# First unit's inverse from blocks of 16 instead of a 32-step substitution, with its V and R turned before its E, and raw W's loads issued first

## The chip, the cores and the metric

The kernel runs on one core of a Trainium2 chip. The metric is device time in microseconds of one execution; several executions are timed and the median is given. The engines are TensorE (PE in the profile, its weight loads PEld), VectorE (DVE), ScalarE (ACT), GpSimd (POOL) and SyncE (SP), which issues most DMAs. Each engine works through its own queue in order, and engines wait for each other through semaphores.

## The reference, cut to what matters

A recurrent attention block (batch 4, 8 heads, 768 tokens, head width 40) is followed by a mixture of four experts over its output, reshaped to 3072 rows of 320.

```python
for t in range(S):
    y[:, :, t] = np.einsum('bhd,bhde->bhe', rt, state)
    Sa = np.einsum('bhde,bhe->bhd', state, at)
    state_decay = state * wt[:, :, None, :] - np.einsum('bhd,bhe->bhde', Sa, bt)
    state = state_decay + np.einsum('bhd,bhe->bhde', vt, kt)
...
x = y.transpose(0, 2, 1, 3).reshape(B * S, H * D)
p = domain_probs / (domain_probs.sum(-1, keepdims=True) + 1e-09)
for e in range(E):
    h = np.maximum(x @ w1[e], 0.0)
    out += p[:, e:e + 1] * (h @ w2[e])
```

All data are float32.

## The kernel before

The sequence is cut into 12 chunks of 64 tokens. A *unit* is one chunk of two of the four batches (partitions 0 to 63 are the tokens of one, 64 to 127 of the other), so there are 24 units; units 0 and 1 are the first chunk. Within a chunk the recurrence is written with matrices: a unit needs the inverse of a unit triangular matrix of 64x64 for each head and batch.

For one unit the work goes in three generators and one function.

`within(q)` (L501) does what needs no state. In order: turn raw W into G, cumulated decays by a scan (L566), pg by TensorE and the reciprocal 1/gp, N and K scaled by it, NT and KT, the products pfe (F, the matrix to be inverted, L664 and L670) and pe (E), then E masked into ET (L686 to L697), then pev and its copies EV (L702 to L708), and for unit 0 last the turned V and R (pVT, pRT, copied by ACT to VT and RT) with the product pc, masked into VC. It yields between these, so that the main program can set other work between two pieces. For units 0 to 3 most of DVE's operations in it are kept in program order.

`substitute(q, ...)` (L717) inverts the two diagonal 32x32 blocks of F for all 8 heads. The blocks are copied side by side, turned into M so that a partition holds one matrix, and 32 columns are eliminated two at a time: sixteen pairs, each a multiplication (L760) and, on DVE, a reduction over three terms (L771), into the tile Z. Units 0 and 1 do it on DVE, later units on POOL. ACT sets the two copies of the unit matrix in Z.

`merge(q)` (L788) turns Z back into Qc and QTc (two transposes on DVE), POOL copies QTc to QT's diagonal, and two products, pY and pQ, with four small ACT copies after each, give the block below the diagonal: the level from 32 to 64.

`step(q, xT)` (L826) has the products with state: psat, pst, pxr, pdy, the result Y and the new state, and pxT, which puts Y into the layout of the mixture. After it the mixture's products follow (ph, po), which read the pieces of w1 (`load_piece`) and w2 (`load_w2`).

The order of PE's instructions is the program's order in the whole first part, as each matmul is kept in program order. `keep_warm(n)` puts n products of the identity with itself into that queue; nothing reads them. On DVE, POOL and SP only what passes through `keep`, `pin`, `keep_in_program_order` or a stated dependence is ordered; the rest is placed by the framework's scheduler. The third weight piece has a stated dependence on unit 0's Y.

The main program (L1217 on) for unit 0: sixteen fillers, W turned, scan, ten fillers, reciprocal, unit 1's G, loads of units 1 and 2 and of weights, N, K, NT, KT, pfe, pe, twenty fillers, the substitution (with the masked E inside), pev, transposes of Z, pVT, pRT, pc, eight fillers, the gate's transposes pp (`normalize`), unit 1's pVT, fifteen fillers, pY, unit 1's pRT, scan and pg, pQ, then `step`.

Raw W is loaded in four DMAs, two issued by SP and two by ACT. Its columns from 48 to 79 are first set to 1.0 in all partitions by a memset (L197, L218); two of the four DMAs write into those columns. PSUM has eight banks: five slots "big" and three "mm".

Of the kernel before, what the change touches and what calls it, by code (L numbers as in the profile page):

```python
# [8 lines left out]
I32 = mybir.dt.int32  # L9
# [24 lines left out]
def kernel(  # L34
# [55 lines left out]
    def noted(ins, name, n=None, i=None):  # L90
        if n is None:
            n = sum(k.startswith(name) for k in made)
        key = f"{name}{n}" if i is None else f"{name}{n}.{i}"
        made[key] = ins
        if key in names:
            stated_order.append(ins)
        return ins

    def keep(ins):

        if not any(ins is x for x in stated_order):
            tc.keep_in_program_order(ins)
# [38 lines left out]
            )  # L141
    mask_up = const.tile([P, L], I32, name="mask_up")

    def dealt(x):

        return x.rearrange("p h (k g) -> p k g h", g=4)
# [46 lines left out]
    def kept(name, shape, n, value=0.0, eng=nc.gpsimd, lo=0):  # L193
        tiles = []
        for i in range(n):
            t = const.tile(shape, FP32, name=f"{name}{i}")
            eng.memset(t[:, :, lo:shape[2]], value)  # L197
            tiles.append(t)
        turn = [0]

        def take():
            turn[0] += 1
            return tiles[(turn[0] - 1) % n]

        return take
# [9 lines left out]
        t = padded["RV"[n % 2], n // 2] = sb.tile([P, H, 64], FP32, name="padded", tag=a_sum)  # L215
        nc.gpsimd.memset(t[:, :, D:64], 0.0)
    PAD = D + D - Q
    raw = {x: kept(f"raw{x}", [P, 2 * NJ, 2 * D], 1, float(x == "W"), nc.vector, PAD) for x in "WARV"}  # L218
    room = {x: const.tile([P, 2 * NJ, 2 * D], FP32, name=f"raw{x}") for x in "BK"}
    raw.update((x, lambda t=t: t) for x, t in room.items())  # L220

# [63 lines left out]
    def load_raw(q, names):  # L285


        moves = []
        for x in names:
            q.n["raw" + x] = t = raw[x]()  # L290
            heads = srcs[x].rearrange("b h t e -> (b h) t e")[q.b[0] * H:(q.b[1] + 1) * H, q.c * L:(q.c + 1) * L, :]
            heads = heads.rearrange("n (x two) e -> x n (two e)", two=2)
            for r in range(2):
                if x in "RV":

                    sets = ((slice(0, 8, 2), slice(r, 16, 4)), (slice(1, 8, 2), slice(3 - r, 16, 4)))
# [136 lines left out]
    def half(s):  # L433
        return slice(64 * s, 64 * s + 64)
# [4 lines left out]
    def of_slot(x, s):  # L439

        return x.rearrange("p (j s) e -> p j s e", s=2)[:, :, s, :]
# [59 lines left out]
    def within(q):  # L501
# [178 lines left out]
        if not q.apart:  # L680
# [24 lines left out]
        ))  # L705
        for i in range(2):
            for p in range(2):
                nc.scalar.copy(out=of_slot(q.EV[half(p)], i ^ p)[:, :, 0:D], in_=pev[i][half(p)])  # L708
        yield

        if q.u == 0:
            pc = causal_scores(turn_rv())
            yield
            masks(pc)
        yield

    def substitute(q, eng, between=None, during=None, first=None):  # L717

# [69 lines left out]
    def merge(q):  # L788


        Qc = sb.tile([P, H, Q], FP32, name="Qc", tag="q", bufs=2)
        QTc = sb.tile([P, H, Q], FP32, name="QTc", tag="q", bufs=2)
        keep(noted(nc.vector.transpose(out=dealt(Qc[:]), in_=q.Z), "Qc", q.u))
        ins = nc.vector.transpose(  # L794
            out=QTc[:].rearrange("p h r -> p (h r)"), in_=Qc[:].rearrange("p h c -> p (h c)"),
        )
        keep(noted(ins, "QTc", q.u))
        q.QT = QTs()
        for i in range(P // Q):
            ins = nc.gpsimd.tensor_copy(out=q.QT[quarter(i), :, quarter(i % 2)], in_=QTc[quarter(i)])  # L800
            tc.keep_in_program_order(ins)
        yield

        def two_heads(name, lhsT, rhs, to):
            p = (of_mixture if q.u == 0 and name == "pY" else big)(name)
            for n in range(NJ):
                for r in range(2):
                    matmul(
                        out=p[half(r), n * 2 * Q:(n + 1) * 2 * Q], lhsT=lhsT[half(r), 2 * n:2 * n + 2, :],
                        rhs=rhs[half(r), 2 * n:2 * n + 2, :], start=True, stop=True,  # L810
                    )
            for r in range(2):
                for y in range(2):
                    src = p[quarter(2 * r + y), 0:H * Q].rearrange("p (n two t) -> p n two t", two=2, t=Q)[:, :, y, :]
                    with sooner(name == "pY"):
                        ins = nc.scalar.copy(out=of_slot(to[quarter(2 * r)], y), in_=src)
# [428 lines left out]
    substitute(units[0], nc.vector, scores_of(0))  # L1245
    run(ws[0], 1)
    set_pick()
    m, s = merge(units[0]), begin_step(0)
    run(m, 1)
    run(ws[0], 1)  # L1250
    keep_warm(8)
    run(norm, 1)
    run(ws[1], 1)
    keep_warm(15)
    load(units[2], "W")
    for x in "VR":
        load_padded(units[2], x)
# [194 lines left out]
    for one, then in [*zip(names, names[1:]), *((f"out{n}", x) for n, x in moved), ("blocks0.3", "VCv1"), ("blocks0.3", "ETc0.0"), ("blocks1.3", "Zu1.0"), ("blocks1.3", "Zu1.3"), *turned_ahead, *in_second, *waits_of_scalar, *ahead_of_merge]:  # L1452
# [31 lines left out]
```

## Time and profile before

| what | value |
|---|---|
| median of 3 runs | 1066.47 us (1066.34 to 1067.45) |
| profiled execution, its own time | 1067.89 us |
| profiled execution, span | 1066.1 us |
| unit 0: last matmuls of pfe and pe start before | 14.8 us |
| unit 0: M transposed | 15.94 to 17.95 us |
| unit 0: first pair of substitution | 20.10 us |
| unit 0: last reduction ends | 30.77 us |
| unit 0: Y on DVE | 41.72 us |
| unit 0: xT copy on ACT | 44.34 us |
| first products ph of the mixture | 45.68 us |

The table's times are from the start of the span, read from the timeline. A time in the span can be compared with another in the span; the time that is measured is the one of the runs, some 1 to 2 us longer than a span.

### The profile page before, as it was taken

The numbers are of one execution on the slowest core, as the hardware profiler recorded it, in microseconds if no ns is written. First come the engines' busy times: TensorE is split into PE (matmuls) and PEld (weight loads), VectorE is DVE, ScalarE is ACT, GpSimd is POOL, SyncE is SP. The second block draws the span as 40 slices with busy tenths as digits, with TensorE's granted clock in tenths as the row PEclk, the third lists the DMA queues.
The fourth block names the chain that finished last, engine by engine and source line by source line (L and its number), as shares of the span: only waits on it lengthen the run. The fifth ranks groups of instructions, "written<-read, shape, count | busy, mean of one in ns | idle before, by whom it ended". The sixth has DMA issues, their size and how long they took to land.

```text
span 1066.1 us, 38525 instructions
## 1 busy us (share of the span) xinstructions
PE 1049.8 (98%) x16022; PEld 942.5 (88%) x16022; DVE 802.2 (75%) x1565; ACT 344.2 (32%) x942; POOL 538.8 (51%) x1322
## 2 busy tenths in 40 slices
PE   7999999999999999999999999999999999999998
PEld 7888888888899999999999999999989998998887
DVE  7787679898778887888788788779788876634343
ACT  3432434333323324233333333232233333221110
POOL 6216777765474574563654744745745646520000
PEclk9999999999999999999999999999999999999999
DMA  6776645344443543453353453454444453121220
GB/s 114 186 211 143 147 95 121 83 98 101 107 103 83 135 109 83 113 131 81 101 135 68 104 147 73 101 115 104 108 114 100 106 109 84 60 83 37 84 78 13
DMA packets 275351, 111.05 MB, mean 104 GB/s; under 512 B 229817, under 2 KB 254953, under 8 KB 275177
## 3 DMA queue, kind: packets, MB, share of 16 engines
q1 hardware_dynamic: 271192, 107.75, 43.3%
q8 instruction: 126, 2.06, 0.8%
q10 hardware_dynamic: 3984, 0.84, 0.4%
q14 instruction: 49, 0.39, 0.1%
HBM read 100.65 MB, written 3.93 MB: 98 GB/s over the span
## 4 chain that ended last, share of the span: by engine, by line
PE 81%; POOL 8%; DVE 5%; issue 2%; DMA 2%; SPq 1%; ACT 1%; DVEq 0%; POOLq 0%; ACTq 0%
PE ph L110 36%; PE p L110 29%; POOL Z L777 5%; POOL Z L760 3%; PE pdy L110 3%; PE prn L110 2%; PE po L110 2%; PE pxr L110 2%; PE psat L110 2%; PE pfe L110 1%; PE pc L110 1%; DVE M L730 1%; PE pev L110 1%; PE pe L110 1%; PE pQ L110 1%
## 5 line engine op out<-in xcount | busy, mean ns | idle before, releaser
L777 POOL TENSOR_TENSOR Z<-Z 128x31 f32<-128x31 f32 (+7 forms) x704 | 265.6, 377 | 55.1
L110 PE MATMUL ph<-xT,w1b 128*128 128x256 f32 (+3 forms) x1536 | 222.3, 374 | 0.5 <-issue 0.5
L110 PE MATMUL ph<-xT,w1a 128*128 128x256 f32 (+3 forms) x1536 | 220.8, 373 | 0.0
L978 ACT ACTIVATE hs<-ph 128x512 f32<-128x512 f32 (+1 forms) x208 | 117.0, 564 | 319.6 <-PE ph L110 317.9
L1104 DVE TENSOR_TENSOR a<-hs 128x512 f32<-128x512 f32 x220 | 155.3, 724 | 81.8 <-ACT hs L978 81.8
L760 POOL TENSOR_TENSOR Z<-M,Z 128x62 f32<-128x62 f32 (+7 forms) x352 | 155.9, 443 | 94.9 <-DVE M L746 69.1
L110 PEld LDWEIGHTS ph<-xT,w1b 128*128 128x128 f32 (+1 forms) x1536 | 168.7, 161 | 27.8 <-issue 7.0
L110 PEld LDWEIGHTS ph<-xT,w1a 128*128 128x128 f32 (+1 forms) x1536 | 167.9, 161 | 28.3 <-issue 7.7
L110 PE MATMUL p<-sums,a 128*128 128x160 f32 x1056 | 164.9, 299 | 0.0
L993 DVE SCALAR_TENSOR_TENSOR osb<-p,gate,osb 128x320 f32<-128x320 f32 (+1 forms) x243 | 107.6, 480 | 69.4 <-PE p L110 66.2
L110 PEld LDWEIGHTS p<-sums,a 128*128 128x128 f32 x1056 | 152.8, 190 | 2.2
L727 POOL COPY below<-F 32x256 f32<-32x256 f32 x48 | 20.7, 432 | 184.0 <-ACT F L670 182.4
L110 PEld LDWEIGHTS p<-w,hs 128*128 128x128 f32 x704 | 98.6, 190 | 8.7 <-issue 7.5
L110 PE MATMUL p<-w,hs 128*128 128x160 f32 x704 | 104.9, 302 | 0.1
L110 PE MATMUL p<-w,a 128*128 128x160 f32 x704 | 102.8, 299 | 0.0
L110 PEld LDWEIGHTS p<-w,a 128*128 128x128 f32 x704 | 98.0, 190 | 0.0
L800 POOL COPY QT<-QTc 32x256 f32<-32x256 f32 x96 | 40.5, 422 | 61.1 <-DVE QTc L794 50.7
L898 ACT COPY RS<-pxr 64x256 f32<-64x256 f32 x88 | 32.3, 367 | 104.6 <-DVE SX L499 76.0
L582 DVE RECIPROCAL gp<-G 128x512 f32<-128x512 f32 x16 | 53.6, 3352 | 0.5
L708 ACT COPY EV<-pev 64x160 f32<-64x160 f32 x96 | 23.1, 286 | 83.6 <-PE pev L110 83.2
L730 DVE STREAM_TRANSPOSE M<-blocks 128x1024 f32<-128x1024 f32 x24 | 47.4, 1974 | 3.4 <-ACT blocks L722 3.3
L670 ACT COPY F<-pfe 128x256 f32<-128x256 f32 x48 | 15.5, 376 | 80.1 <-PE pfe L110 77.9
(167 smaller groups left out, 1419.3 us busy)
## 6 DMA issues: line engine op xcount, KB each, us to landing
w1a<-in_moe_w_dram SPq DMA_DIRECT2D x37, 512.0 KB
w1b<-in_moe_w_dram SPq DMA_DIRECT2D x37, 512.0 KB
w<-in_moe_w_dram SPq DMA_DIRECT2D x4, 1280.0 KB
w1a<-in_moe_w_dram SPq DMA_DIRECT2D x74, 64.0 KB
w1b<-in_moe_w_dram SPq DMA_DIRECT2D x74, 64.0 KB
out_dram<-osb SPq DMA_DIRECT2D x45, 80.0 KB
rawW<-in_w_dram SPq DMA_DIRECT2D x48, 72.0 KB
natV<-in_v_dram SPq DMA_DIRECT2D x42, 80.0 KB
```

What stands on the lines that cost most here:

```text
L110: return stated(nc.tensor.matmul(**k))
L582: pin(noted(nc.vector.reciprocal(out=gp[:], in_=G[:, :, 1:L + 1]), "1/gp", q.u))
L708: nc.scalar.copy(out=of_slot(q.EV[half(p)], i ^ p)[:, :, 0:D], in_=pev[i][half(p)])
L727: tc.keep_in_program_order(nc.gpsimd.tensor_copy(out=q.below[quarter(i)], in_=q.F[quarter(i), :, 0:Q]))
L730: ins = nc.vector.transpose(out=M[:], in_=cols)
L760: ins = eng.tensor_tensor(out=Z[:, 1:3, 0:n, j + 1:Q], in0=M[:, j:j + 2, None, j + 1:Q].to_broadcast([P, 2, n, m]), in1=Z[:, here, 0:n, j: ...
L777: eng.tensor_tensor(out=z[:, 0], in0=z[:, 0], in1=z[:, x], op=ALU.add)
L800: ins = nc.gpsimd.tensor_copy(out=q.QT[quarter(i), :, quarter(i % 2)], in_=QTc[quarter(i)])
L898: nc.scalar.copy(out=RS[half(s), x ^ s::2], in_=prs[x][half(s)].rearrange("p (j i) t -> p j i t", i=2),)
L978: ins = nc.scalar.activation(out=h[:, i * HF // 2:(i + 1) * HF // 2, 0:n], in_=ph[i][:], func=ACTF.Relu,)
L993: ins = nc.vector.scalar_tensor_tensor(out=to, in0=p, scalar=sc, in1=to, op0=ALU.mult, op1=ALU.add)
L1104: ins = nc.vector.tensor_tensor(out=t[:], in0=x, in1=y, op=op)
```

## The change

Only unit 0 is treated differently: `substitute_small` takes the place of `substitute`. It inverts the four 16x16 diagonal blocks (eight column pairs in eight steps of multiplication and reduction on tiles half as long), and `merge` puts a level before the one it has: W = inner * QTc, then QTc and Qc get a product added (32x32 products, one for each head and quarter of the partitions). `set_bands` makes the masks and scales that this needs, and half of the unit matrix; they lie in a tile `small`. V and R of unit 0 are turned, and pc computed, before E is masked; the fillers are dealt out anew (4, 16, 12, 18 in place of 20, 8, 15). Raw W gets a tile whose ones are set only in the partitions where no DMA writes those columns. The gate's normalization and two weight pieces stand later in the program.

```diff
+    T = Q // 2
+    small = sb.tile([P, 512], FP32, name="small", tag="step", bufs=3)
...
+    def set_bands():
+        nc.vector.reduce_sum(out=of_rows, in_=ident[:].rearrange("p (i b r) -> p b i r", i=2, r=T), axis=AX.XY)
+        nc.vector.tensor_copy(out=band, in_=of_rows[:, :, None].to_broadcast([P, 4, T]))
+        nc.vector.reduce_sum(out=lane_x, in_=ident[:].rearrange("p (a x h) -> p x a h", x=2, h=H), axis=AX.XY)
+        nc.vector.tensor_copy(out=lanes_of_second, in_=lane_x[:, 1:2, None].to_broadcast([P, 1, T]))
+        diag = diagf[:, 0:T].rearrange("p (k g) -> p k g", g=2)[:, :, :, None]
+        nc.vector.transpose(out=unit_small, in_=diag.to_broadcast([P, T // 2, 2, 2 * H]))
...
-    raw = {x: kept(f"raw{x}", [P, 2 * NJ, 2 * D], 1, float(x == "W"), nc.vector, PAD) for x in "WARV"}
+    raw = {x: kept(f"raw{x}", [P, 2 * NJ, 2 * D], 1, 0.0, nc.vector, PAD) for x in "ARV"}
+    raw_w = const.tile([P, 2 * NJ, 2 * D], FP32, name="rawW")
+    for i in (1, 3):
+        nc.vector.memset(raw_w[Q * i:Q * i + Q, :, PAD:D + Q], 1.0)
...
     tc.keep_in_program_order(ins)
+    set_bands()
     for n, move in enumerate(load_raw(units[0], "W")):
...
+        if q.u == 0:
+            VT = turn_rv()
+            yield
+            pc = causal_scores(VT)
+            yield
+
         ET = ETs()
...
         if q.u == 0:
-            pc = causal_scores(turn_rv())
-            yield
             masks(pc)
...
+    def substitute_small(q, first, second):
+        K = T // 2
+        blocks = sb.tile([P, H, Q], FP32, name="blocks")[:, :, 0:T]
+        keep(nc.vector.tensor_copy(out=blocks, in_=q.F[:, :, 0:T]))
+        for n in range(1, 4):
+            keep(nc.vector.copy_predicated(
+                out=blocks, mask=band[:, n:n + 1, :].to_broadcast([P, H, T]), data=q.F[:, :, n * T:n * T + T],
+            ))
+        run(first)
+        q.below = belows()
...
+        q.inner = sb.tile([P, H, Q], FP32, name="inner", tag="step", bufs=3)
+        nc.gpsimd.memset(q.inner[:, :, T:Q], 0.0)
+        for i in range(P // Q):
+            ins = nc.gpsimd.affine_select(
...
+        for x in (0, 3):
+            nc.scalar.copy(out=z[:, x], in_=unit_small[:, :, 0:T])
+        M = sb.tile([P, Q, Q], FP32, name="M")
+        cols = blocks.rearrange("p h c -> p c h")[:, :, None, :].to_broadcast([P, T, 4, H])
+        keep(nc.vector.transpose(out=M[:, 0:T], in_=cols))
+        m = M[:, 0:T, 0:T]
+        keep(nc.vector.copy_predicated(
+            out=m, mask=lanes_of_second.to_broadcast([P, T, T]), data=M[:, 0:T, T:Q],
+        ))
...
+        for j in range(0, T, 2):
+            n, w_ = j // 2 + 1, T - 1 - j
...
+        run(second)
+        ins = nc.scalar.activation(out=q.Z[:, :, T:Q], in_=z[:, 0], func=ACTF.Copy, scale=lane_x[:, 1:2])
+        tc.add_manual_dep(ins.ins, made["EVc0.3"].ins.name, BEHIND, reason="stated order of ScalarE")
+        keep(nc.vector.tensor_scalar(out=q.Z[:, :, 0:T], in0=z[:, 0], scalar1=lane_x[:, 0:1], scalar2=None, op0=ALU.mult))
...
     def merge(q):
...
+        def of_blocks(name, lhsT, rhs):
+            p = of_mixture(name)[:, 0:H * Q].rearrange("p (h c) -> p h c", c=Q)
+            for h in range(H):
+                for i in range(P // Q):
+                    o = quarter(i)
+                    matmul(out=p[o, h, :], lhsT=lhsT[o, h, :], rhs=rhs[o, h, :], start=True, stop=True)
+            return p
+
+        if q.u == 0:
+            W = sb.tile([P, H, Q], FP32, name="inner_Q", tag="step", bufs=3)
+            tc.keep_in_program_order(nc.scalar.copy(out=W[:], in_=of_blocks("pW", q.inner, QTc)))
+            yield
+            for name, to, lhsT, rhs in (("pQTc", QTc, Qc, W), ("pQc", Qc, W, Qc)):
+                p = of_blocks(name, lhsT, rhs)
+                keep(nc.vector.tensor_tensor(out=to[:], in0=p, in1=to[:], op=ALU.add))
         q.QT = QTs()
...
     load_w2(order_of(-1)[0])
-    load_piece()
-    load_piece()
     run(ws[0], 2)
-    keep_warm(20)
+    keep_warm(4)
+    run(ws[0], 1)
+    keep_warm(16)
+    run(ws[0], 1)
+    keep_warm(12)
...
-    substitute(units[0], nc.vector, scores_of(0))
-    run(ws[0], 1)
+    substitute_small(units[0], scores_of(0), scores_of(0))
     set_pick()
+    keep_warm(18)
     m, s = merge(units[0]), begin_step(0)
     run(m, 1)
+    run(ws[1], 1)
     run(ws[0], 1)
-    keep_warm(8)
-    run(norm, 1)
-    run(ws[1], 1)
-    keep_warm(15)
+    run(m, 1)
     load(units[2], "W")
...
     run(m)
     go(load_raw(units[2], "A"))
+    load_piece()
+    load_piece()
     run(s, 3)
+    run(norm, 1)
     run(ws[1], 1)
```

The two stated orders of DVE that named unit 0's blocks go as well (ahead of unit 1's V copy and of the copy of E).

More of the change, by code (lines that the diff above doesn't have):

```diff
@@ L142 @@
     mask_up = const.tile([P, L], I32, name="mask_up")
+    T = Q // 2
+    small = sb.tile([P, 512], FP32, name="small", tag="step", bufs=3)
+    unit_small = small[:, 0:T // 2 * Q].rearrange("p (k r) -> p k r", r=Q)
+    band = small[:, 256:320].bitcast(I32).rearrange("p (b r) -> p b r", r=T)
+    lanes_of_second = small[:, 320:336].bitcast(I32)[:, None, :]
+    lane_x, of_rows = small[:, 336:338], small[:, 340:344]
+    def set_bands():
[5 more added lines that the diff above has]
+        nc.vector.transpose(out=unit_small, in_=diag.to_broadcast([P, T // 2, 2, 2 * H]))
     def dealt(x):
@@ L217 @@
     PAD = D + D - Q
-    raw = {x: kept(f"raw{x}", [P, 2 * NJ, 2 * D], 1, float(x == "W"), nc.vector, PAD) for x in "WARV"}
+    raw = {x: kept(f"raw{x}", [P, 2 * NJ, 2 * D], 1, 0.0, nc.vector, PAD) for x in "ARV"}
+    raw_w = const.tile([P, 2 * NJ, 2 * D], FP32, name="rawW")
+    for i in (1, 3):
+        nc.vector.memset(raw_w[Q * i:Q * i + Q, :, PAD:D + Q], 1.0)
+    raw["W"] = lambda: raw_w
     room = {x: const.tile([P, 2 * NJ, 2 * D], FP32, name=f"raw{x}") for x in "BK"}
@@ L707, in within @@
             for p in range(2):
-                nc.scalar.copy(out=of_slot(q.EV[half(p)], i ^ p)[:, :, 0:D], in_=pev[i][half(p)])
+                ins = nc.scalar.copy(out=of_slot(q.EV[half(p)], i ^ p)[:, :, 0:D], in_=pev[i][half(p)])
+                noted(ins, "EVc", q.u, 2 * i + p)
         yield
         if q.u == 0:
-            pc = causal_scores(turn_rv())
-            yield
             masks(pc)
         yield
+    def substitute_small(q, first, second):
[8 more added lines that the diff above has]
+        q.below = belows()
+        for i in (1, 3):
+            tc.keep_in_program_order(nc.gpsimd.tensor_copy(out=q.below[quarter(i)], in_=q.F[quarter(i), :, 0:Q]))
+        q.inner = sb.tile([P, H, Q], FP32, name="inner", tag="step", bufs=3)
+        nc.gpsimd.memset(q.inner[:, :, T:Q], 0.0)
+        for i in range(P // Q):
+            ins = nc.gpsimd.affine_select(
+                out=q.inner[quarter(i), :, 0:T], in_=q.F[quarter(i), :, quarter(i % 2)][:, :, 0:T],
+                pattern=[[0, H], [0, T]], compare_op=ALU.is_ge, fill=0.0, base=-T, channel_multiplier=1,
+            )
+            tc.keep_in_program_order(ins)
+        Z = sb.tile([P, 4, Q // 4, Q], FP32, name="Z")
+        flat = Z[:].rearrange("p x k r -> p (x k r)")
+        z = flat[:, 0:4 * K * T].rearrange("p (x k r) -> p x k r", k=K, r=T)
+        for x in (0, 3):
[7 more added lines that the diff above has]
+        ))
+        pairs = M[:, 0:T].rearrange("p (c two) r -> p c two r", two=2)[:, :, :, 0:T]
+        cells = M[:, 0:T].rearrange("p c r -> p (c r)")
+        keep(nc.vector.memset(cells[:, Q + 1::2 * (Q + 1)], 0.0))
+        by_second = z[:, 1:3].rearrange("p x k r -> p (x k r)")[:, 0:K * T].rearrange("p (k r) -> p k r", r=T)
+        keep(nc.vector.tensor_tensor(
+            out=by_second, in0=pairs[:, :, 1, :],
+            in1=cells[:, 1::2 * (Q + 1)][:, :, None].to_broadcast([P, K, T]), op=ALU.mult,
+        ))
+        keep(nc.vector.tensor_tensor(out=pairs[:, :, 0, :], in0=pairs[:, :, 0, :], in1=by_second, op=ALU.add))
+        for j in range(0, T, 2):
+            n, w_ = j // 2 + 1, T - 1 - j
+            here = 3 * (j // 2 % 2)
+            nc.vector.tensor_tensor(
+                out=z[:, 1:3, 0:n, j + 1:T], in0=M[:, j:j + 2, None, j + 1:T].to_broadcast([P, 2, n, w_]),
+                in1=z[:, here, 0:n, j:j + 2].rearrange("p k x -> p x k")[:, :, :, None].to_broadcast([P, 2, n, w_]),
+                op=ALU.mult,
+            )
+            now = z[:, :, 0:n, j + 1:T]
+            terms = now[:, 0:3] if here == 0 else now[:, 1:4]
+            nc.vector.tensor_reduce(
+                out=now[:, 3 - here], in_=terms.rearrange("p x k r -> p k r x"), op=ALU.add, axis=AX.X,
+            )
+        odd, even = (z[:, x].rearrange("p k (r four) -> p k r four", four=4)[:, :, :, 1:3] for x in (3, 0))
+        nc.vector.tensor_copy(out=even, in_=odd)
+        q.Z = flat[:, 4 * K * T:4 * K * T + K * Q].rearrange("p (k r) -> p k r", r=Q)
+        run(second)
+        ins = nc.scalar.activation(out=q.Z[:, :, T:Q], in_=z[:, 0], func=ACTF.Copy, scale=lane_x[:, 1:2])
+        tc.add_manual_dep(ins.ins, made["EVc0.3"].ins.name, BEHIND, reason="stated order of ScalarE")
+        keep(nc.vector.tensor_scalar(out=q.Z[:, :, 0:T], in0=z[:, 0], scalar1=lane_x[:, 0:1], scalar2=None, op0=ALU.mult))
@@ L792, in merge @@
         QTc = sb.tile([P, H, Q], FP32, name="QTc", tag="q", bufs=2)
-        keep(noted(nc.vector.transpose(out=dealt(Qc[:]), in_=q.Z), "Qc", q.u))
+        place = Qc[:].rearrange("p h (x c) -> p c x h", x=2) if q.u == 0 else dealt(Qc[:])
+        keep(noted(nc.vector.transpose(out=place, in_=q.Z), "Qc", q.u))
         ins = nc.vector.transpose(
@@ L1451 @@
     in_second = [("Zr1.14", "out0"), ("out0", "Zm1.16")]
-    for one, then in [*zip(names, names[1:]), *((f"out{n}", x) for n, x in moved), ("blocks0.3", "VCv1"), ("blocks0.3", "ETc0.0"), ("blocks1.3", "Zu1.0"), ("blocks1.3", "Zu1.3"), *turned_ahead, *in_second, *waits_of_scalar, *ahead_of_merge]:
+    for one, then in [*zip(names, names[1:]), *((f"out{n}", x) for n, x in moved), ("blocks1.3", "Zu1.0"), ("blocks1.3", "Zu1.3"), *turned_ahead, *in_second, *waits_of_scalar, *ahead_of_merge]:
         tc.add_manual_dep(made[then].ins, made[one].ins.name, BEHIND, reason="stated order of VectorE")
```

## The prediction

> **What bounds it now.** First I read the busy shares on the page, then the waits of the PE queue, then the timeline of the first 46 us. Columns in the timeline are start, duration, engine, line, operation, out<-in, count, and in brackets the idle time before it with what ended it.
>
> ```profile
> PE 1049.8 (98%) x16022; PEld 942.5 (88%) x16022; DVE 802.2 (75%) x1565; ACT 344.2 (32%) x942; POOL 538.8 (51%) x1322
> q8 instruction: 126, 2.06, 0.8%
> ```
>
> PE is idle for 1066.1 - 1049.8 = 16.3 us, and the waits listed up to 46 us add up to 7.8 of them. From 41 us on, unit 0's results and the experts' weights keep PE full, so what the change gains or loses until unit 0's pxT is passed on to the end. The path to be watched is therefore PE's own queue, fillers ("warm") included, since its order is written out.
>
> ```profile
> 1.76 6.11 PE L110 MATMUL warm<-ident 128*128 128x128 f32 x32 [1.76 <-POOL ident L128]
> 8.14 0.66 PE L113 MATMUL pg<-ident,G 128*128 128x128 f32 x4 [0.27 <-DVE G L566]
> ...
> 14.41 0.65 ACT L670 COPY F<-pfe 128x256 f32<-128x256 f32 x2 [0.31 <-PE pfe L110]
> ...
> 14.78 4.73 PE L110 MATMUL warm<-ident 128*128 128x128 f32 x40
> ...
> 19.44 0.81 PE L110 MATMUL pev<-VC,ET 64*64 64x40 f32 x32
> ...
> 28.74 3.51 PE L110 MATMUL warm<-ident 128*128 128x128 f32 x30
> ...
> 31.48 0.45 DVE L794 STREAM_TRANSPOSE QTc<-Qc 128x256 f32<-128x256 f32 x1
> 31.84 1.18 DVE L566 TENSOR_TENSOR_SCAN G<-G,first 128x512 f32<-128x512 f32 x1
> ...
> 32.18 0.68 PE L110 MATMUL pY<-QTc,below 64*64 64x64 f32 x16
> ...
> 32.96 1.07 ACT L816 COPY Yq<-pY 32x128 f32<-32x128 f32 x4 [2.90 <-PE pY L110]
> ...
> 33.28 0.60 PE L113 MATMUL pg<-ident,G 128*128 128x128 f32 x4
> ...
> 33.81 0.95 PE L110 MATMUL pQ<-Yq,Qc 64*64 64x64 f32 x16
> ```
>
> To be seen: twenty fillers fill 14.78 to 19.44, 0.233 us each. The last fifteen end at 32.2, just as QTc comes (31.93): fillers and substitution are level at pY. Unit 1's pg stands in PE's queue between pY and pQ and needs unit 1's scan.
>
> **Raw W first, bands.** The second rawW issue on SP moves from 2.27 to about 1.4, so G's transposes (5.64, released by a DMA) could start near 4.8. set_bands adds two sums, two copies and a transpose on DVE: about 2x0.25 + 0.17 + 0.1 + 0.45 = 1.2 us (rows of total, mask_up, gl, unit_cols), hidden in DVE's 1.88 idle us before G; without that cover the same 1.2 is on the path. But pg cannot start before the sixteen fillers end at 7.87: gain 0.27, and pe starts at 13.91, F is ready at 14.8.
>
> **Shorter substitution.** On DVE: copy 0.22, three predicated copies 128x128 at about 0.25 (0.38 for 128x256), M transpose half of 2.01, predicated copy 0.38, memset 0.07, two operations at 0.24: 2.9 with gaps. A pair of steps now costs 0.47 (16 elements) to 0.67 (108); eight pairs of 16 to 72 elements give 0.49+0.53+0.57+0.59+0.59+0.55+0.51+0.47 = 4.3, against 10.7 for the sixteen (20.10 to 30.77). Z is done at 22.4. Its scaling on ACT is put behind EV's copies, which follow pev; the W and Yq copies queue behind it on ACT.
>
> **PE's queue.** From pe's end at 14.51: fifty fillers at 0.233 = 11.65; pVT and pRT 0.95; pc 0.6; pev 0.74 (19.44 to pVT at 20.18): pW starts at 28.45. pev comes at 23.5, EV's copies end at 25.3 (1.8 after pev, as before), the scaling at 25.6, Qc and QTc (0.63+0.04+0.45) at 26.8. So the fillers, not the substitution, release pW; 1.4 us of the saving stand unused, and nothing of DVE's 6.4 reaches the path but the start of this queue. Fillers at 0.229 to 0.240 (the rows of 30 and 20) move it by 0.3. POOL's below, inner (four selects at 0.28, 6.61/24, and a memset) and ET selects end about 21, covered by pev's place; VT's and RT's copies (2.27) by the sixteen fillers.
>
> **The new level.** Products of 32x32 are not in the trace. pfe's sixteen 64-wide calls show as 32 matmuls in four-tile batches, 0.51 us for eight batches; pst, 40 wide, has the same pace. Between half that pace (width counts) and double, I take the same: 32 calls are sixteen batches, 0.93 us, and 0.36 more until a reader starts (pY: 0.78 to the Yq copy, of which 0.46 to its last matmul). pW 28.45, W copy 29.74 to 30.1 (0.38), pQTc 30.15, add 31.44 to 31.84, pQc to 32.05, its add 32.37 to 32.75, pY 32.2: level with before. But unit 1's scan, kept in order, now stands behind both adds: 32.75 to 33.95, so pg 34.0 and pQ 34.55 instead of 33.81: **+0.74**. Half pace makes this -0.8, double pace +3.6.
>
> A rule speaks against this level: the Trainium skill, "TensorEngine Tiling (Array Packing)", Restrictions and Gotchas, says that different row tiles cannot use one PSUM bank at the same time, and of_blocks writes four row tiles into one bank. The trace does not bear it out: pY's two row tiles share a bank, and its 16 matmuls start two by two.
>
> **Code for PE.** The page's 32044 PE instructions over 126 packets are 254 a packet. This stop has no releaser:
>
> ```profile
> 41.01 0.30 PE L110 MATMUL pdy<-SX,n_tok 64*64 64x104 f32 x1 [0.86 <-issue]
> ```
>
> Counting back 256 (a call shows as two loads and two matmuls): pdy 80, pxr 64, pst 64, psat 48, to about 35.9; another 256 to 23.65 in pc, another to 14.1. The DMA view has a packet of the instruction queue in 38.0 to 38.9 and none in 36.0 to 38.4; one in 24.0 to 24.6; one in 14.9 to 15.6. So a block is asked for when the one before it is entered, and came 5 us later at 35.9, where DMA was busiest; from the packet to the resumption 2.5, hence 3 at 23.65. In the new order the borders lie in the twelve fillers (22.2), in pW's last quarter (29.2), and 256 later in pQc: pW 30, pVT 8, pQTc 128, pQc 90, at 31.7. That is 2.5 us for a block that takes 3 to 5: a wait of 0.5 to 2.5. DMA share there is 0.79 to 0.88, nearer to 1.05 at 35.9 than to 0.19 after 23.65: I take 4.2, a wait of **1.7**, which holds up pQc, pY, both adds and what hangs on them. The next borders fall at pxr and pc, some 5 us apart, so pdy's stop goes: **-0.86**.
>
> **Moved work.** pp (0.65) goes into PE's 0.61 wait for SX; its gate copy is 0.24 on ACT; without that cover 0.65. The weight pieces already waited on SP for Y (42.50 after 41.72), ahead of rawA, rawB, rawK; nothing is used from them before 56.2. Masks move into DVE's idle time before the adds. I put these at 0.
>
> **Sum.** +0.74 + 1.7 - 0.86 = +1.6 us, the 0.27 and the fillers already in it. The profiled execution took 1067.89 (span 1066.1 and 1.8 around it) and would take 1069.5; the median of the runs is 1066.47, which gives **1068.1**.
>
> **Rivals.**
> B, code comes in time: the block takes 3 us and waits 0.3 to 0.5, pdy's stop is gone: +0.74+0.5-0.86 = +0.4, **1066.9**. For it: most borders show no stop. Against: dense small products are where the one stop is. The Trainium skill, "Runtime: NRT & Kernel Launch", Instruction fetch mechanics, holds that crossing a 16 KiB border is mostly hidden; by that rule the time is this one, and the stop at 41.01 is a row against it.
> C, the substitution decides as it says: PE is at pW by the time Z's chain ends without EV (22.4+0.25+1.12+0.25 = 24.1), 4.3 earlier: 1068.1 - 4.3 = **1063.8**. For it: DVE's sum. Against: it needs fillers under (24.1-14.51-2.29)/50 = 0.146 us.
> D, slower, the clock. Columns: busy time of PE, PEld, DVE, ACT, POOL (and count), granted clock, DMA share, GB/s.
>
> ```profile
> 9.98:13.39 3.41, 2.08 (x18) 1.71 (x16) 3.38 (x5) 1.72 (x5) 3.00 (x9) 1.00 0.70 116
> 20.22:23.63 3.41, 1.41 (x22) 1.04 (x19) 3.03 (x12) 3.17 (x10) 0.00 (x0) 1.00 0.63 118
> 23.63:27.04 3.41, 3.41 (x36) 3.29 (x37) 3.14 (x9) 0.00 (x0) 0.00 (x0) 0.50 0.19 49
> 30.46:33.87 3.41, 3.41 (x42) 3.06 (x41) 3.31 (x10) 0.86 (x4) 1.77 (x3) 1.00 0.88 264
> ```
>
> PE busy for 1.41 of 3.41 was followed by 3.41 us at half clock, 2.08 was not. My new order leaves about 2.0 in 30.46 to 33.87; under some 1.8 half a window is lost, 1.7 us: **1069.8**.
> E: the four row tiles take turns: 64 matmuls at 0.058 are 3.7 us for each of the three products, 2.8 more than the sum has, 8.4 in all: **1076**. No row speaks for it, only the rule cited above.
>
> **Chances.** Forecast 0.46, B 0.20, C 0.17, D 0.14, E 0.03. A difference under 0.2% (2.1 us) is about what a measurement of this kernel cannot tell from none, so slower begins at 1068.6. The forecast's own range is 1066.9 to 1069.7, and nearly half of it (0.24) lies beyond. Faster: C, 0.17. Within: 0.22 + 0.20 = 0.42. Slower: 0.24+0.14+0.03 = 0.41. The range 1064.3 to 1070.5 leaves out C's fast half, E and the tails.
>
> **What would show it.** Right: pW directly behind the last filler near 28.4 with QTc a microsecond older; a PE stop without releaser in pQc or pY; scan behind two adds and pg waiting for it; no stop in pdy. Wrong: PE waiting for QTc before pW, products much off 0.93 us, unit 0's xT copy earlier than 44.34.

## The result, and the profile after

The changed kernel takes 1073.41 us (median of 6 runs, 1072.16 to 1074.79), the kernel before on the same chip 1067.62 (6 runs, 1066.34 to 1068.56): ratio 1.0056, 95% interval 1.0043 to 1.0069. It is slower by 5.8 us, where 1.6 were forecast, and lies above the range. The profiled execution is the fastest of the six, 1072.16 with a span of 1070.4: 4.3 us more than the profiled one of before.

The page's busy line of the changed kernel:

```profile
PE 1053.2 (98%) x16228; PEld 945.7 (88%) x16228; DVE 797.4 (74%) x1561; ACT 343.6 (32%) x942; POOL 537.8 (50%) x1327
```

PE idles for 17.2 us (1070.4 - 1053.2), 0.9 more than before, and is busy for 3.4 more. Most of the loss is made in one place of the timeline (columns as in the prediction):

```profile
7.43 0.60 PE L113 MATMUL pg<-ident,G 128*128 128x128 f32 x4
...
13.55 0.65 ACT L691 COPY F<-pfe 128x256 f32<-128x256 f32 x2 [0.31 <-PE pfe L110]
...
22.95 0.68 PE L110 MATMUL pev<-VC,ET 64*64 64x40 f32 x32
23.56 4.29 PE L110 MATMUL warm<-ident 128*128 128x128 f32 x36
...
25.77 0.45 DVE L884 STREAM_TRANSPOSE QTc<-Qc 128x256 f32<-128x256 f32 x1
27.77 0.75 PE L110 MATMUL pW<-QTc,inner 32*32 32x32 f32 x64
29.05 0.72 PE L110 MATMUL pQTc<-inner_Q,Qc 32*32 32x32 f32 x62
...
29.62 0.68 PE L110 MATMUL pQc<-Qc,inner_Q 32*32 32x32 f32 x41
29.98 0.42 DVE L903 TENSOR_TENSOR QTc<-pQTc,QTc 128x256 f32<-128x256 f32 x1 [3.10 <-PE pQTc L110]
35.10 0.53 PE L110 MATMUL pQc<-Qc,inner_Q 32*32 32x32 f32 x21 [4.80 <-issue]
35.56 1.12 PE L110 MATMUL pY<-QTc,below 64*64 64x64 f32 x16
35.68 0.42 DVE L903 TENSOR_TENSOR Qc<-pQc,Qc 128x256 f32<-128x256 f32 x1 [5.28 <-PE pQc L110]
36.02 1.21 DVE L587 TENSOR_TENSOR_SCAN G<-G,first 128x512 f32<-128x512 f32 x1
37.52 1.06 PE L113 MATMUL pg<-ident,G 128*128 128x128 f32 x4
38.51 1.12 PE L110 MATMUL pQ<-Yq,Qc 64*64 64x64 f32 x16
...
48.07 0.48 ACT L1042 COPY xT<-pxT 128x384 f32<-128x384 f32 x1 [0.81 <-PE pxT L110]
```

Until 30.3 all goes as planned or better: Z's transposes end at 26.22, the fillers at 27.85, pW follows at once, and 64 products of 32x32 are started in some 0.56 us (0.75 with the last one's end). Then PE stands in the middle of pQc, after 43 of its 64 matmuls, for 4.80 us, waiting for nothing that the profile shows. Behind the stop the same operations take longer: pY 1.12 where it took 0.68, pg 1.06 where it took 0.60. The windows say why (columns: PE, PEld, DVE, ACT, POOL, granted clock, DMA share, GB/s):

```profile
30.46:33.87 3.41, 0.00 (x0) 0.00 (x0) 0.00 (x0) 0.00 (x0) 1.57 (x4) 0.91 1.10 338
33.87:37.28 3.41, 2.18 (x40) 1.99 (x40) 1.56 (x3) 0.48 (x2) 0.00 (x0) 0.50 0.65 116
```

In the first stretch PE did nothing and DMA was full; from 33.3 to 40.1 PE's granted clock was 0.5. The copy xT comes at 48.07 where it came at 44.34: 3.7 of the span's 4.3 us are lost by then.

### The profile page after: what moved, and what is told of

Read it like the earlier page. It is cut to its first block, busy times and chain, and to the rows that moved or that the text cites. A ratio compares the mean times of both kernels' runs of the same rounds, so it can differ in the third digit from the quotient of the medians.

```text
span 1070.4 us, 38944 instructions
## 1 busy us (share of the span) xinstructions
PE 1053.2 (98%) x16228; PEld 945.7 (88%) x16228; DVE 797.4 (74%) x1561; ACT 343.6 (32%) x942; POOL 537.8 (50%) x1327
## 4 chain that ended last, share of the span: by engine, by line
PE 83%; POOL 10%; DVE 3%; issue 2%; ACT 1%; DMA 1%; SPq 0%; POOLq 0%; DVEq 0%
PE ph L110 35%; PE p L110 29%; POOL Z L866 6%; POOL Z L849 3%; PE pdy L110 3%; PE prn L110 2%; PE po L110 2%; PE pxr L110 2%; PE psat L110 2%; PE pfe L110 1%; PE pc L110 1%; PE warm L110 1%; PE pev L110 1%; PE pe L110 1%; PE pQ L110 1%
## 5 line engine op out<-in xcount | busy, mean ns | idle before, releaser
L866 POOL TENSOR_TENSOR Z<-Z 128x31 f32<-128x31 f32 (+7 forms) x704 | 272.3, 387 | 55.1
L849 POOL TENSOR_TENSOR Z<-M,Z 128x62 f32<-128x62 f32 (+7 forms) x352 | 148.2, 421 | 94.6 <-DVE M L835 68.9
```

The source lines that it names most:

```text
L849: ins = eng.tensor_tensor(out=Z[:, 1:3, 0:n, j + 1:Q], in0=M[:, j:j + 2, None, j + 1:Q].to_broadcast([P, 2, n, m]), in1=Z[:, here, 0:n, j: ...
L866: eng.tensor_tensor(out=z[:, 0], in0=z[:, 0], in1=z[:, x], op=ALU.add)
```

## The experiments

Each ran beside the kernel before on the same chip; ratios are to its runs.

**The stop is code.** To show it without the change, the kernel before got 96 products of 32x32 that nothing reads, ahead of pY:

```diff
     keep_warm(15)
+    extra = of_mixture("extra")
+    for n in range(3 * H):
+        for i in range(P // Q):
+            o = quarter(i)
+            ins = matmul(out=extra[o, 0:Q], lhsT=ident[o, quarter(i)], rhs=ident[o, quarter(i)], start=True, stop=True)
+            tc.keep_in_program_order(ins)
```

> The kernel before, with 96 products of 32x32 that nobody reads set into PE's queue between the last filler and pY: PE's share of the new level by itself, without its adds and copies and without the new order of the scan. Theory 1: the products take 3x0.56 = 1.7 us of PE, and a border of the code lies near the start of pY, asked for about 2.5 us earlier; PE stops there without a releaser for 2.5 to 5 us, and the time rises by 3 to 6 us. Rival (it is the adds, copies and the order behind them that cost, not the code): no stop, +1.7 us at most.

It took 1076.18 (one run; before 1067.51): 8.7 us more, above the 3 to 6 expected; 10.2 us at half clock follow the stop. Its timeline has the stop inside products that depend on nothing:

```profile
38.93 0.42 PE L110 MATMUL extra<-ident 32*32 32x32 f32 x11 [5.06 <-issue]
```

If all PE records (matmuls, loads and the waits for semaphores between them) are counted from the start of the span, the first one behind this stop is number 962. It is 962 in the changed kernel too, and behind the stop of 0.86 in pdy of the kernel before. Three different products stop at one count, which speaks for a border in PE's instructions and against anything in the data. Borders 256 records apart put the one before at 706.

The DMA view of the changed kernel shows what PE waits for (columns: packets, MB, share of the 16 engines). From 28.3 to 32.5 there is data alone; from 32.5 to 33.6 one packet of the instruction queue:

```profile
q1 hardware_dynamic: 924, 1.33, 95.2%
...
q8 instruction: 1, 0.02, 6.0%
```

If the next block is asked for when PE enters a block, it had these times to come (start of the record behind each border and of the packet, from the traces; the three kernels with QTc transposed stop at 1218, the others at 962):

| kernel | border before, us | packet begins after | behind the border, us | between | stop |
|---|---|---|---|---|---|
| before | 36.06 | 2.40 | 41.01 | 4.95 | 0.86 |
| before, 96 products more | 32.60 | 3.33 | 38.93 | 6.33 | 5.06 |
| before, one cast more | 35.73 | 2.73 | 40.92 | 5.19 | 1.10 |
| before, new tile of raw W | 37.65 | 0.52 | 41.38 | 3.73 | none |
| changed | 28.19 | 4.32 | 35.10 | 6.91 | 4.80 |
| changed, no new level | 38.71 | 2.79 | 43.98 | 5.27 | 0.88 |
| changed, weights late | 34.45 | 2.11 | 39.03 | 4.58 | 2.49 |
| changed, w2 late | 28.19 | 3.01 | 33.70 | 5.51 | 3.43 |
| changed, casts on POOL | 29.05 | 5.26 | 36.90 | 7.85 | 5.78 |
| changed, casts on POOL, w2 late | 29.03 | 2.52 | 33.93 | 4.90 | 2.77 |
| changed, pieces put right | 27.40 | 1.96 | 31.60 | 4.20 | 1.81 |
| QTc transposed, weights late | 33.62 | 4.39 | 40.77 | 7.15 | 2.86 |
| the same, weights early | 33.89 | 4.29 | 40.81 | 6.92 | 2.63 |
| the same, w1 early, w2 late | 33.50 | 2.31 | 38.21 | 4.71 | 0.42 |

So where PE stopped, a block took 4.2 to 7.9 us from the border before to PE's going on. In each of the thirteen PE goes on 1.2 to 1.5 us after the end of the packet; in the one kernel without a stop the packet ended 2.0 us before PE was at the border. What differs is how long the packet takes to begin. (At record 450, under fillers, it begins up to 0.8 us before PE is there in eight of the profiles, so the asking can run somewhat ahead of PE.) The kernels in the other rows are told below.

Leaving the new level out moves the same count into pdy:

```diff
         if q.u == 0:
+            yield
+        if False:
             W = sb.tile([P, H, Q], FP32, name="inner_Q", tag="step", bufs=3)
```

> The changed kernel without the new level: pW, its copy, pQTc, pQc and both adds are left out, so the blocks of 16 are not joined to 32 for the first unit. Theory 1: 384 instructions fewer between the fillers and pY, no stop of code there; pY follows the fillers at 27.9 instead of 35.56, and the time falls by 7 to 9 us against the changed kernel. Rival (the stop comes anyway a block later): the fall is below 4 us.

There is no stop before pY, and one of 0.88 in pdy, at record 962. But the time was 1070.74 (one run), only 2.7 us less than the changed kernel's and not the 7 to 9 expected: pY starts at 34.98, not at 27.9. Another line shows the reason; see the cast below.

**What makes the stop long.** First the weights were moved out of the way, to behind pQ:

```diff
     load_probs()
-    load_piece()
-    load_piece()
-    load_w2(order_of(-1)[0])
...
     run(m)
+    load_piece()
+    load_piece()
+    load_w2(order_of(-1)[0])
     go(load_raw(units[2], "A"))
```

> The changed kernel with the loads of the first two weight pieces and the first w2 moved in the program from before the products of the new level to behind pQ. Theory 1: PE's stop of 4.8 us in pQc is a code block that comes late because it is asked for while these 2.5 MB are on the DMA queues. Then the stop shrinks to at most 1.5 us, no half clock follows, and the time falls by 4 to 6 us, to 1067 to 1069.5 where the changed kernel has 1073.4. Rival: the stop belongs to the dense small products whatever the DMAs do; then it stays at 4 us or more and the time stays within 1 us of 1073.4. Second rival: the weights now come late for ph or po; then PE waits for a DMA there and the time is 1073 or more.

The stop was 2.49 us instead of 4.80, but the 1.5 and the 1067 to 1069.5 expected were both missed: the time was 1075.82 (4 runs, 1071.68 to 1077.78; ratio 1.0066, 1.0043 to 1.0089). In the profiled one (1077.78) unit 0's G was turned 6.2 us late, at 10.57: again the cast. And 10.2 us at half clock follow the stop. With w2 alone behind unit 0's Y:

```diff
-    load_w2(order_of(-1)[0])
     run(ws[0], 2)
...
     go(load_raw(units[2], "A"))
+    load_w2(order_of(-1)[0])
     load_piece()
...
+    tc.add_manual_dep(made["wtwo0"].ins, made["Y0.0"].ins.name, AFTER, reason="weights not beside code")
```

> The changed kernel with one DMA moved: the first expert's w2 (1280 KB, issued at 26.2 in the profiled run, when all else of the weights is under way) waits for unit 0's Y, as the third weight piece does. Nothing of PE's order or of its code's borders changes. Theory (the block for pQc's border is asked for in pW near 28.3 and its packet comes at 32.5 to 33.6 because the DMA engines are full with w2): the packet comes 1.5 to 3 us earlier, the stop in pQc shrinks from 4.8 to between 1.5 and 3.3, and the time falls to 1068 to 1071. Rival (the fetch takes as long as it takes, whatever else is transferred): stop and time stay, 4.5 us or more and 1072.5 to 1074.5.

```profile
33.70 0.54 PE L110 MATMUL pQc<-Qc,inner_Q 32*32 32x32 f32 x21 [3.43 <-issue]
```

The stop shrank by 1.4, just short of what was expected: the packet of the instruction queue lies at 31.2 to 32.4 instead of 32.5 to 33.6, with the same record (962) behind it. The time did not follow, 1068 to 1071 being expected: 1076.32 (4 runs), although the profiled one took 1073.14; there the half clock lasted 13.7 us, twice as long as after the change, and po waited 0.9 us for w2.

**The cast.** In the profile of the kernel without the level, DVE at the start:

```profile
3.66 6.67 DVE L154 CAST small<-small 128x64 int32<-128x64 f32 x1
3.73 6.60 DVE L155 TENSOR_REDUCE small<-ident 128x2 f32<-128x128 f32 x1
3.92 6.41 DVE L158 STREAM_TRANSPOSE small<-masks_f 128x256 f32<-128x256 f32 x1
9.51 0.76 POOL L188 MEMSET sums<- 128x768 f32 x1
...
10.57 0.76 DVE L344 STREAM_TRANSPOSE G<-rawW 128x256 f32<-128x256 f32 x2
...
13.12 1.11 PE L113 MATMUL pg<-ident,G 128*128 128x128 f32 x4 [6.16 <-DVE G L587]
```

set_bands' first cast, a copy of 64 columns, ends at 10.33, when POOL's unbroken row of memsets (3.31 to 10.27) has just ended, and all of DVE's queue stands behind it: the later entries begin early and end with it. The profile with the weights late has the same, 6.67 us. In the profiled run of the changed kernel the same cast took 0.39:

```profile
3.64 0.39 DVE L154 CAST small<-small 128x64 int32<-128x64 f32 x1
3.71 0.32 DVE L155 TENSOR_REDUCE small<-ident 128x2 f32<-128x128 f32 x1
...
4.39 0.77 DVE L344 STREAM_TRANSPOSE G<-rawW 128x256 f32<-128x256 f32 x2
```

The Trainium skill, "SBUF — State Buffer", SBUF: two separate sides, describes a pair of ports that GpSimd shares with some of VectorE's operations as an exclusive lock: who starts first has it for the whole instruction, and the other is blocked fully. The rows fit such a lock, and go further: the cast was passed over through some twenty memsets one behind the other, 6.3 us. That this cast is one of those operations, and why it is not held each time, no run here shows.

To see whether this is part of the loss, both casts were put on POOL, where they fall behind most of the memsets:

```diff
-        nc.vector.tensor_copy(out=band, in_=of_rows[:, :, None].to_broadcast([P, 4, T]))
+        nc.gpsimd.tensor_copy(out=band, in_=of_rows[:, :, None].to_broadcast([P, 4, T]))
...
-        nc.vector.tensor_copy(out=lanes_of_second, in_=lane_x[:, 1:2, None].to_broadcast([P, 1, T]))
+        nc.gpsimd.tensor_copy(out=lanes_of_second, in_=lane_x[:, 1:2, None].to_broadcast([P, 1, T]))
```

> The changed kernel with the two small casts of set_bands on POOL instead of DVE; POOL takes them behind its row of memsets, near 9.5 us. Theory: the cast on DVE (0.39 us in the profiled run of the changed kernel, 6.67 us in two of its variants) is at times held until POOL's row of memsets ends, and everything behind it on DVE with it; without it G is transposed near 4.4 us in every execution, the sum and the transpose of set_bands take 0.3 to 0.45 us each, the runs spread less and the median is 1071 to 1072.5, about the best run of the changed kernel (1072.16). The stop without releaser in pQc stays (4 to 5 us). Rival 1: the stall belongs to set_bands whole (its sum or its transpose are held as well): a stall of 6 us still shows in DVE before G, and the median stays 1072.5 to 1075. Rival 2: the stop in pQc alone makes all of the loss: median 1073.4 as before.

1073.63 (4 runs, 1072.05 to 1075.51; ratio 1.0062, 1.0046 to 1.0078): as the changed kernel, above the 1071 to 1072.5 of the theory. G was turned at 4.38, the stop in pQc was 5.78 us in the profiled run (1075.51), with 10.2 us at half clock behind. So the cast is not what cost the 5.8 us; the second rival was right. A cast like it in the kernel before:

```diff
+    unread = sb.tile([P, 512], FP32, name="unread", tag="step", bufs=3)[:, 0:64].bitcast(I32)
+    tc.keep_in_program_order(nc.vector.tensor_copy(
+        out=unread.rearrange("p (b r) -> p b r", r=16), in_=masks_f[:, 0:4, None].to_broadcast([P, 4, 16])))
```

> The kernel before with one cast more on DVE, 128x64 from SBUF to SBUF, right behind the transpose of unit_cols; nothing reads its result. DVE waits there for raw W anyway (1.88 us). Theory (the cast is held by POOL's row of memsets when it comes in the middle of it): in the executions in which it is held it ends near 10.3 us instead of 4.0, G is transposed at 10.4 instead of 5.64, and the time is 3 to 5 us longer: median 1067.5 (never held) to 1072 (always held). Rival (the stall has another cause than cast beside memsets): the cast takes 0.2 us, and the time is 1067.5 within 0.5.

1066.97 (10 runs; ratio 1.000, 0.999 to 1.001), the cast at 3.69 took 0.20 us. That is the rival's outcome: the cast was not held in the profiled run, and none of the ten times is 3 us longer. So a cast beside the memsets need not be held, and what decides it stays open. What tells more is the kernel with w2 late, whose 1076.32 was unexplained, with the casts on POOL as well:

> The kernel with only w2 moved behind unit 0's Y, which took 1073.14 in its profiled run (cast on DVE not held, stop 3.43) and 1076.2 to 1077.4 in three others, and now also with the two casts of set_bands on POOL. Theory (the three slow ones were runs in which DVE's cast was held for 6 us by POOL's memsets): no run is above 1074.5, the median is 1070 to 1073.5, and the stop in pQc is 2 to 3.5 us. Rival (the spread comes from how long the block of code takes and which clock windows fall behind it, and the late w2 costs more than it gives): the runs spread over 3 us or more and the median stays at 1075 to 1077.

1071.20 (7 runs, 1069.49 to 1074.42; ratio 1.0043, 1.0027 to 1.0059), stop 2.77 us. With the casts off DVE the median falls by 5.1 us from the 1076.32 of the same kernel with them on DVE, and no run is above 1074.5: held casts are the likely cause of its three runs above 1076, though none of these was profiled. Against the kernel with the casts alone on POOL (1073.63), w2's late load takes the median down by 2.4, though the runs overlap.

**Raw W alone.** The kernel before, with the new tile for raw W and nothing else:

```diff
-    raw = {x: kept(f"raw{x}", [P, 2 * NJ, 2 * D], 1, float(x == "W"), nc.vector, PAD) for x in "WARV"}
+    raw = {x: kept(f"raw{x}", [P, 2 * NJ, 2 * D], 1, 0.0, nc.vector, PAD) for x in "ARV"}
+    raw_w = const.tile([P, 2 * NJ, 2 * D], FP32, name="rawW")
+    for i in (1, 3):
+        nc.vector.memset(raw_w[Q * i:Q * i + Q, :, PAD:D + Q], 1.0)
```

> The kernel before with the new tile of raw W alone, so that its loads are issued first. The changed kernel's trace had pe 0.86 us earlier. If that came of raw W alone, this kernel is 0.7 to 0.9 us faster than before; if PE's first fillers bind as I had put it, 0.27 or less. Both are under what the rounds tell apart, so the place of pe (14.18 before, 13.32 changed) decides: 13.3 or 13.9.

1067.33 (10 runs; ratio 0.9999, 0.9989 to 1.0008). pe starts at 13.60, halfway between the two places that were to decide. Then pev waits 0.76 for ET, the half clock behind 23.8 lasts 6.8 us where it was 3.4, and xT comes at 44.67: this part alone is worth nothing, since the masked E is late next.

**Putting the pieces right.** Casts on POOL, first weights behind pQ, unit 1's pRT and scan ahead of the level, twelve fillers instead of eighteen ahead of pW (casts and weights as shown above):

```diff
-    keep_warm(18)
+    keep_warm(12)
...
     run(ws[0], 1)
+    run(ws[1], 2)
     run(m, 1)
...
     run(m, 1)
-    run(ws[1], 2)
     run(ws[0])
```

> The changed kernel with the two casts on POOL, the first two weight pieces and w2 loaded after pQ, unit 1's pRT and scan ahead of the new level, and twelve fillers instead of eighteen ahead of pW. Theory (what was lost is the stop for code, the half clock behind it, and the scan behind the adds): the stop in pQc is 2.5 us or less (2.49 with the late weights alone), pg does not wait for the scan; from the best run 1072.16 that is -2.3 for the stop, -1.4 for the fillers, -0.7 for the scan: 1067 to 1068.5, less by up to 1.7 if no window runs at half clock. Rival (the DMA load has nothing to do with the stop): the stop stays 4.5 us or more and the time is 1069.5 or more.

1067.58 (10 runs, 1066.07 to 1069.03; ratio 1.0005, 0.9996 to 1.0014): all but the whole loss is back, as expected; the share of each piece was not measured. The stop is 1.81 us, pg follows pY without a wait, and PE's clock stays at 1.00 through the stretch.

Then the border itself was moved: the product pQTc was left out, and QTc is the transpose of the finished Qc, with five fillers to cover it.

```diff
-            for name, to, lhsT, rhs in (("pQTc", QTc, Qc, W), ("pQc", Qc, W, Qc)):
-                p = of_blocks(name, lhsT, rhs)
-                keep(nc.vector.tensor_tensor(out=to[:], in0=p, in1=to[:], op=ALU.add))
+            keep(nc.vector.tensor_tensor(out=Qc[:], in0=of_blocks("pQc", W, Qc), in1=Qc[:], op=ALU.add))
+            keep(nc.vector.transpose(
+                out=QTc[:].rearrange("p h r -> p (h r)"), in_=Qc[:].rearrange("p h c -> p (h c)"),
+            ))
...
     run(m, 1)
+    keep_warm(5)
```

> As the kernel before this one in the list, and the product pQTc is left out: QTc is made by transposing the finished Qc on DVE (0.45 us) instead, and five fillers stand between pQc and pY. The result is the same matrix. Theory (64 matmuls and their 64 loads fewer in the dense stretch move the border of PE's code to the first matmuls of pQ, some 4.5 us behind the border in pW, and the block is there by then): no stop without releaser over 1 us before psat, pY near 30, pQ near 32.5 where it was 33.8 in the kernel before; 1064 to 1066.5. Rival (the stop comes wherever the next border lies): a stop of 2 to 5 us moves into pQ, and the time is 1067 to 1071.

No stop up to psat, which starts at 33.17 where it started at 35.16 before the change: the border at 962 now falls into psat, where the theory had put it into pQ, and PE takes 6.8 us from 706 to there. But 256 records later, at 1218, in pdy:

```profile
40.77 0.47 PE L110 MATMUL pdy<-VC,k_tok 64*64 64x104 f32 x4 [2.86 <-issue]
```

1069.60 (10 runs; ratio 1.0021, 1.0011 to 1.0030). The rival was right about the time, but not about the place: the block asked for in psat meets the late weights, where the DMA share is 0.89 to 1.05. With the weights back at their early place:

> The kernel with QTc transposed from Qc, with the first weights back at their old place ahead of the stretch. Theory: the stop of 2.9 us in pdy goes, because w1 and w2 are over when the block for it is asked for near 33; the block for pQ is asked for near 27, under w2, and a stop of 0.5 to 3 us may come at pQ instead; 1066 to 1069. Rival (the border in pdy stops whatever the load): stop of 2 us or more in pdy, 1069 to 1071.

1068.78 (one run). The stop in pdy stays, 2.63 us: this expectation failed, though the time lies in its range. w2 was issued at 27.9 there, and unit 2's loads behind it dragged on to 41.9, so the DMA engines were hardly freer (share 0.92 from the border to the packet). With w1 early and w2 behind Y:

> The kernel with QTc transposed from Qc, w1's first two pieces at their old early place, and w2 behind unit 0's Y. Theory: neither the block for pQ (asked for near 27) nor that for pdy (asked for near 33) has w2 beside it: stops under 1 us in all until pxT, pQ near 32, pxT 2 us or more earlier than in the kernel before, no window at half clock: 1063.5 to 1066, faster than the kernel before. Rival (w2 is then late for po, or the DMA load only moves): a stop of 2 us or more at a border, or a wait of po for w2: 1067 to 1070.

1065.69 (10 runs, 1064.03 to 1067.34; ratio 0.9986, 0.9975 to 0.9996): faster than both kernels, by 1.2 us over the one before, with an interval that ends close to 1. Its timeline:

```profile
26.32 0.75 PE L110 MATMUL pW<-QTc,inner 32*32 32x32 f32 x64
...
28.03 0.75 PE L110 MATMUL pQc<-Qc,inner_Q 32*32 32x32 f32 x64
28.71 1.38 PE L110 MATMUL warm<-ident 128*128 128x128 f32 x10
29.29 0.45 DVE L904 STREAM_TRANSPOSE QTc<-Qc 128x256 f32<-128x256 f32 x1
30.03 0.68 PE L110 MATMUL pY<-QTc,below 64*64 64x64 f32 x16
...
38.21 0.34 PE L110 MATMUL pdy<-VC,k_tok 64*64 64x104 f32 x4 [0.42 <-issue]
...
41.79 0.48 ACT L1045 COPY xT<-pxT 128x384 f32<-128x384 f32 x1 [0.75 <-PE pxT L110]
```

The stop at record 1218 is 0.42, PE's clock is 1.00 from 5.6 us on, and xT comes 2.55 us before that of the kernel before. Of these, 1.3 are left in the span (1064.8 against 1066.1). Later PE waits 1.0 us for weights, which the kernel before does not (0.8 for a piece of w1 at 84.9, 0.2 for w2 in po): this much of the rival came true. And it stops without releaser for 0.60 in pxr near 145 and 0.62 in pQ near 235, where the one of before has 0.41 in pxr near 146 and 0.50 in ph near 245.

## Why the prediction was wrong

**The step that failed is "Code for PE": a wait of 1.7, bounded by 0.5 to 2.5.** Place and cause were right: the stop came in pQc, after 87 of its 128 loads and matmuls, where the 90th was forecast. The size was not: 4.80 us, and 5.06, 5.78, 3.43, 2.49 in other kernels. The block was taken to need 3 to 5 us from its asking, and 4.2 was chosen between two rows; it needed 6.9. Of these, 2.6 from the packet's start to PE's going on are as forecast (2.5). The wait for the packet to begin is what was mis-sized: 1.7 of the 4.2 (4.2 - 2.5), but 4.3 in the trace. The other 0.4 of the 3.1 too few is that PE needed 2.1 us from border to border where 2.5 was forecast.

The wait was put between two rows by the DMA share, and the share does not tell it: from the border to the packet it was 1.00 in the kernel before, where the packet began after 2.4 us, and 0.94 in the changed kernel, where it began after 4.3. What was under way does: three pairs of kernels differ in w2's place alone, and with w2 late the stop is 3.43 instead of 4.80, 2.77 instead of 5.78, 0.42 instead of 2.63, each time because the packet begins 1.3 to 2.7 us sooner. These are single profiles, but the two stops of the same kind with w2 early, 4.80 and 5.78, lie above both with w2 late. In which way a large transfer delays the packet stays open. Even the one row under a full DMA (5 us at a share of 1.05) would have given a stop of 2.5: the bounds came from single blocks of one kernel, and the blocks of thirteen stops show 4.2 to 7.9. The Trainium skill's rule ("Runtime: NRT & Kernel Launch", Instruction fetch mechanics) that a crossing is mostly hidden, cited for rival B, is not borne out at this border; over the whole span it is, with at most three stops of over 0.4 us at borders in any profile.

**Rival D came on top instead of in its place.** The clock was a case of its own at 1.7 us. But the half clock follows from the stop: the clock drops at 33.28, 3.0 us into it, for 6.8 us; of the 3.41 us before, PE was busy for 0.44. In the other profiles, too, each of the stops of 2.49 us and more was followed by 3.4 to 13.7 us at half clock (eight of eight), and none of the five of 1.81 and less. From pY to pQ it took 2.95 where 2.35 (34.55 - 32.20) were forecast. The sum should have had the two as one term.

**Terms that were too dear.** Products: 0.56 us each, not 0.93; the four row tiles neither wait for each other nor run at the pace of pfe's, so rival E is out. (The Trainium skill's rule on row tiles in one PSUM bank, cited there, has no price here.) Without the stop pQc would have been done near 30.5 instead of 32.05. pg came 0.71 earlier, not 0.27: the sixteen fillers themselves ended 0.28 earlier (7.59 for 7.87).

**Right.** Fillers release pW, not the substitution (27.77 against 26.22 for QTc): rival C is out. pdy's stop is gone. Unit 1's scan stands behind both adds, but in the changed kernel pg shows no wait for it: the scan ended at 37.23, while PE at half clock had pRT to do until 37.7. pg did wait for it in two kernels with a shorter stop, 0.56 with the weights late and 0.42 with w2 late and the casts on POOL; taking the scan ahead was one of the pieces that brought the loss back. What is gained or lost at xT is passed on, as the path had it: from xT to the end of the span it is 1021.2 to 1023.1 us in all fourteen profiles. The waits of the kernel before up to 46 us add up to 7.5, not to 7.8; no term used them.

**set_bands, "hidden":** in the profiled run it was. The 6.3 us for which its cast can be held were in none of the cases, although POOL's row of memsets stood in the profile of before. In the changed kernel's own median no cost of it shows; in the variant with w2 late it is the likely cause of 5.1 us.

Against its own profile the forecast's +1.6 became +4.3: the stop +3.1 over the forecast, products and earlier start -1.5, half clock from pY to pQ +0.6, which makes 3.8 at xT (3.7 measured), and 0.6 after xT. The six runs go further up (+5.8 in the medians); the profiled one was the fastest. The mean granted clock is 0.997 in it and 0.993 in the slowest, which fits a longer half clock; how long the stop was in the other five is not known.

## What to carry to other kernels

A stretch of many small PE instructions is priced by its instruction blocks first and by its arithmetic second: count where the borders of 256 fall, and what the DMA engines carry in the 4 to 8 us ahead of each. If a stop without releaser appears, fewer instructions in the stretch or one large transfer moved out of it were worth more here than the fillers or the arithmetic, and a stop of 2.5 us or more is to be charged with the half clock behind it. Copies on VectorE at the start of a program are better not put beside a row of GpSimd memsets.

## What the runs showed that was not expected

- PE's stops without releaser of 0.42 us and more up to 60 us stand at record 962 or 256 later, in all thirteen profiles that have one, whatever product lies there; they last from 0.42 to 5.78 us, and the block needed 4.2 to 7.9 us. PE goes on 1.2 to 1.5 us after the packet of the instruction queue ends.
- A cast of 64 columns on VectorE, usually 0.2 to 0.4 us, took 6.67 beside GpSimd's row of memsets in two profiles of the five that had such a cast there; in which executions it is held stays open.
- 64 matmuls of 32x32 from four row tiles into one PSUM bank start within 0.56 us, 0.009 us apart.
